# Attention fused with a squared-ReLU MLP: three low bits of every second weight piece on GpSimd, its products on VectorE, a third float32 unit

## The chip, the cores and the metric

The kernel runs on one core of a Trainium2 chip. The metric is the device time of one execution in microseconds (us). Of the kernel before, three runs were timed: 588.53, 588.9 and 590.05 us, with a median of 588.9.

## The reference, cut to what matters

```
scores = q @ k.T / 8;  masked causally;  a = softmax(scores)          # B 4, H 8, S 576, D 64
local  = a @ v
mem    = (phi(q) @ M_prev) / (phi(q) @ z_prev + 1e-6)                 # phi(x) = elu(x) + 1
attn   = g * mem + (1 - g) * local                                    # g = sigmoid(beta), by head
x      = attn as 2304 tokens x 512
out    = (relu(x @ w_in) ** 2) @ w_out                                # 512 -> 2048 -> 512
```

`w_in` and `w_out` come as 64-bit floats and the rest as 32-bit floats. The result is float32.

## The kernel before, in words

**Weights.** The weights are loaded as 32 pieces of 128 rows x 512 columns (`wsrc`, L140 to L146); four pieces of `w_in` and four of `w_out` alternate. Each 64-bit number comes as two 32-bit words. `split_weight` (L156) turns a piece into a float32r high part and a low part in five steps: VectorE shifts the low word right by 29, which leaves its three top bits (L162); ScalarE rebases the exponent of the high word (L163); VectorE shifts that by three and puts the three bits in (L164); ScalarE copies the high part (L167); VectorE subtracts to get the low part (L168). Pieces lie in scratch of their own (`raw`), in two halves of 256 columns (`xw`), or in tiles borrowed from the tokens (`hw`).

**First tokens.** `first_tokens` (L224) computes the first 64 tokens of each of the four batches in two groups. The table `TE` (L65) names the engine of five of its elementwise steps for each group (`d` VectorE, `p` GpSimd): L272, L274, L279, L288 and L294. Each works on 128x512 numbers.

**Attention.** The rest is done in units of one batch and one pair of heads, in an order fixed in `order` (L792). In the first two batches a unit covers two of the four query tiles, afterwards all four. For a unit `loads` (L332) brings keys, queries and values (`kd`, `qm`, `vv`; one buffer of `kd` and one of `vv`). TensorE makes the scores (L465), VectorE adds the mask and takes the row minimum (L484), ScalarE the exponential (L504).
The first `NEF` = 2 units are `full`: TensorE transposes the probabilities in float32 (L519), ScalarE copies them out (L524), and TensorE multiplies them by `vv` in float32 (L563). In all others `vv` is scaled and split into two float16 halves (L398 to L415), the probabilities are split into float16 halves too (L542, L544), a DMA transposes them (L548), and TensorE multiplies in float16 (L569 to L574), after which VectorE adds the halves (L576). L584 adds the memory part, L595 stores to a scratch in DRAM. `TAGS`, `a` and `aT` give the buffers of the split path. The transposes of a `full` unit share their two PSUM buffers (tag `up`) with the MLP.

**MLP.** `moe(n)` (L695) works on a block of 256 tokens in eight steps `j`. A step makes `up` by 24 matmuls of 256 columns (L719 to L721), takes ReLU and square into `r` (one buffer), a high part `gh` (L728 on ScalarE for the first four blocks, L730 on VectorE for the others) and the low part `gl` (L731 on GpSimd), and the step before it multiplies by `w_out` with 12 matmuls of 512 columns (L709 to L711). Block 0 needs the first tokens; the others need their attention rows (`prefetch`, L609). The last two blocks go together in `moe_pair` (L650), with 512 columns and its own `gl` on GpSimd (L677).

**Order.** `ORD` (L79) merges unit 0 with the first 13 weight steps, then units 1 to 3 with the other weight steps and `moe(0)`; the other units and blocks follow. A planner in the framework places the instructions on each engine by its own estimate of their times, so the order within an engine isn't that of the code. Each engine then works its queue in order. All DMAs of the kernel are issued by the queue of SP.

Of the kernel before, what the change touches and what calls it, by code (L numbers as in the profile page):

```python
# [8 lines left out]
F32 = mybir.dt.float32  # L9
F32R = mybir.dt.float32r  # L10
F16 = mybir.dt.float16
BF16 = mybir.dt.bfloat16
U32 = mybir.dt.uint32
AF = mybir.ActivationFunctionType
ALU = mybir.AluOpType
AX = mybir.AxisListType
# [19 lines left out]
PM = 'pd'  # L36
FX = 'dd'
GHN = 4
VMIN = 2.0**-80
NEF = 2  # L40
NES = 6
PXT = 'up'
PXE = 'aa'
# [18 lines left out]
SGROUP = {2: [[(2, 0, 320), (1, 0, 192)]], 1: [], 3: [[(3, 0, 448), (4, 0, 64)]], 4: [[(4, 64, 576)]]}  # L62
STG = [(9, 'hlx'), (8, 'hlx'), (3, 'hlx'), (0, 'hlx')]
XF = 0
TE = ['dd', 'dp', 'pp', 'pp', 'pp']  # L65
TC = 'aa'
TW = 2 * NP * 6 * D
GB = 2
# [21 lines left out]
def fused_kernel(ctx: ExitStack, tc: tile.TileContext, t0_d, zt_d, kk_d, qv_d, beta, w_in, w_out, out):  # L90
    nc = tc.nc
    w_in = w_in.bitcast(U32)
    w_out = w_out.bitcast(U32)
    cp = ctx.enter_context(tc.tile_pool(name="cp", bufs=1))
# [14 lines left out]
        out=mask, in_=mask, pattern=[[-1, MW]], compare_op=ALU.is_ge, fill=-1e30, base=448, channel_multiplier=1  # L109
# [13 lines left out]
    def gates():  # L123
        nc.scalar.activation(gpm, gpm, AF.Exp, scale=-1.0)
        nc.vector.tensor_scalar(out=gpm, in0=gpm, scalar1=1.0, scalar2=None, op0=ALU.add)
        nc.vector.reciprocal(gpm, gpm)
        nc.vector.reciprocal(gi, gm)
        nc.vector.tensor_scalar(out=gm, in0=gm, scalar1=-1.0, scalar2=1.0, op0=ALU.mult, op1=ALU.add)
        nc.vector.reciprocal(gm, gm)
        nc.vector.tensor_scalar(out=gs, in0=gm, scalar1=SC, scalar2=None, op0=ALU.mult)  # L130

        for b in range(GB):
            nc.vector.tensor_copy(gpb[:, b * NP : (b + 1) * NP], gp)
        nc.vector.tensor_scalar(out=g1b, in0=gpb, scalar1=-1.0, scalar2=1.0, op0=ALU.mult, op1=ALU.add)
# [18 lines left out]
    def w_out_op(f, part):  # L153
        return wt[8 * (f // 4) + 4 + f % 4][:, part, :]

    def split_weight(n):  # L156
        for rw, c0, c1 in raw.pop(n):
            rw = rw.rearrange("p (n t) -> p n t", t=2)
            u0, u1 = rw[:, :, 0], rw[:, :, 1]
            f1 = u1.bitcast(F32)  # L160
            hi, lo = wp[n][:, 0, c0:c1], wp[n][:, 1, c0:c1]
            nc.vector.tensor_scalar(out=u0, in0=u0, scalar1=29, scalar2=None, op0=ALU.logical_shift_right)  # L162
            nc.scalar.activation(f1, f1, AF.Prelu, scale=2.0**-111, alpha=-(2.0**32))  # L163
            nc.vector.scalar_tensor_tensor(  # L164
                out=u1, in0=u1, scalar=3, in1=u0, op0=ALU.logical_shift_left, op1=ALU.bitwise_or
            )
            nc.scalar.copy(hi, f1)  # L167
            nc.vector.tensor_tensor(out=lo, in0=f1, in1=hi.bitcast(F32), op=ALU.subtract)  # L168

    def load_weight(n, pool):  # L170
        raw[n] = []
        if pool == "x":
            for c in range(2):
                t = mo.tile([P, DM], F32, tag="x", name="xw", bufs=XB).bitcast(U32)
                raw[n].append((t, c * 256, (c + 1) * 256))
        elif pool in ("h", "l"):
            t = mo.tile([P, NK, BLK], F32, tag="x" + pool, name="hw", bufs=2)
            raw[n].append((t.rearrange("p a b -> p (a b)").bitcast(U32), 0, 512))
        elif pool == "e":
            t = at.tile([P, 2, S], F32, tag="e", name="ew", bufs=EB)  # L180
            raw[n].append((t.rearrange("p a b -> p (a b)").bitcast(U32)[:, :1024], 0, 512))
        else:
            u = wp[n].shape[2] // 512
            raw[n].append((pool.tile([P, 1024 * u], U32, name=f"raw{n}"), 0, 512 * u))
            if u == 2:
# [38 lines left out]
    def first_tokens(tp, ahead):  # L224
        me, ze, se, xe, ye = ([nc.gpsimd if c == "p" else nc.vector for c in t] for t in TE)
        xh = mo.tile([P, NK, BLK], F32R, tag="xh", name="xh", bufs=2)
# [39 lines left out]
        def phi(g):  # L266
# [3 lines left out]
            t2 = tp.tile([P, GN], F32, tag="t2", name="t2", bufs=2)  # L270
            nc.scalar.activation(f, qn, AF.Exp)
            me[g].tensor_scalar(out=f, in0=f, scalar1=1.0, scalar2=None, op0=ALU.min)  # L272
# [8 lines left out]
        def softmax(g):  # L281
# [6 lines left out]
            xe[g].tensor_tensor(out=e, in0=e, in1=t1[:, :, None].to_broadcast(bc), op=ALU.subtract)  # L288
            nc.scalar.activation(e, e, AF.Exp)
            nc.vector.reduce_sum(out=t1, in_=e, axis=AX.X)  # L290
# [38 lines left out]
    dp = ctx.enter_context(tc.tile_pool(name="dp", bufs=1, space=bass.MemoryType.DRAM))  # L329
# [15 lines left out]
    def attention(b, p, tiles, ld, after, early, sfull, full):  # L345
# [31 lines left out]
        w = slice(qa, qb)  # L377
        nc.scalar.activation(pe[:, w], q_raw[:, w], AF.Exp)
        ph = pe if sfull else q_raw
        if PHI and not sfull:  # L380
            nc.scalar.activation(q_raw[:, w], q_raw[:, w], AF.Relu)
            nc.vector.scalar_tensor_tensor(
# [10 lines left out]
        if not full:  # L393
# [10 lines left out]
            nc.vector.tensor_scalar(  # L404
                out=vy, in0=vy, scalar1=VMIN, scalar2=2.0**-VEXP, op0=ALU.max, op1=ALU.mult
            )
# [288 lines left out]
    def moe(n):  # L695
        b, blk = blocks[n]
        xh, xl = xq.pop()
        pend = []
        acc = []

        def down(j, gh, gl):
            if j == 0:
                for t in range(2):
                    acc.append(ps.tile([P, DM], F32, tag="acc", name="oacc", bufs=2))
            last = j == NF // 2 - 1
            for u, t in [(u, t) for t in range(2) for u in range(2)] if last else [(u, t) for u in range(2) for t in range(2)]:
                f = 2 * j + u
                ts = slice(t * P, (t + 1) * P)
                nc.tensor.matmul(acc[t], gh[:, u, ts], w_out_op(f, 0), start=f == 0, stop=False)  # L709
                nc.tensor.matmul(acc[t], gh[:, u, ts], w_out_op(f, 1), start=False, stop=False)  # L710
                nc.tensor.matmul(acc[t], gl[:, u, ts], w_out_op(f, 0), start=False, stop=f == NF - 1)  # L711

        for j in range(NF // 2):
            need(1 + 8 * (j // 2 + 1))
            up = ps.tile([P, 2, BLK], F32, tag="up", name="up", bufs=2)
            for u in range(2):
                f = 2 * j + u
                for k in range(NK):
                    nc.tensor.matmul(up[:, u, :], w_in_op(f, k, 0), xh[:, k, :], start=k == 0, stop=False)  # L719
                    nc.tensor.matmul(up[:, u, :], w_in_op(f, k, 0), xl[:, k, :], start=False, stop=False)  # L720
                    nc.tensor.matmul(up[:, u, :], w_in_op(f, k, 1), xh[:, k, :], start=False, stop=k == NK - 1)  # L721
            r = mo.tile([P, 2, BLK], F32, tag="r", name="r", bufs=RB)
            gh = mo.tile([P, 2, BLK], F32R, tag="gh", name="gh", bufs=GHB)
            gl = mo.tile([P, 2, BLK], F32R, tag="gl", name="gl", bufs=GLB)
            nc.scalar.activation(r, up, AF.Relu, scale=WSC)  # L725
            nc.scalar.activation(r, r, AF.Square)
            if n < GHN:
                nc.scalar.copy(gh, r)  # L728
            else:
                nc.vector.tensor_copy(gh, r)  # L730
            nc.gpsimd.tensor_tensor(out=gl, in0=r, in1=gh.bitcast(F32), op=ALU.subtract)  # L731
            pend.append((j, gh, gl))
            yield
            if n == NBLK - 3 and j in (3, PJ):
                if j == 3:
                    xq.append(pair_tiles())
                pair_prefetch(xq[-1], int(j == PJ))
                yield
            elif j == PJ and n + 1 < NBLK:
                assert n > 0 or last  # L740
                xq.append(prefetch(*blocks[n + 1], *last))
                last.clear()
                yield
            if len(pend) > 1:
                down(*pend.pop(0))
                yield
        for x in pend:
            down(*x)
            yield
        for t in range(2):  # L750
            o = mo.tile([P, DM], F32, tag="x", name="o", bufs=XB)
            nc.scalar.activation(o, acc[t], AF.Copy, scale=WSC)
            if b is None:
                for u in range(2):
                    r0 = (2 * t + u) * S
                    nc.sync.dma_start(out[r0 : r0 + D, :], o[u * D : (u + 1) * D])
            else:
                r0 = b * S + QT[1 + 2 * blk + t][0]
                nc.sync.dma_start(out[r0 : r0 + P, :], o)
        yield  # L760
# [19 lines left out]
    def need(n):  # L780
        while wn[0] < n:
            next(wg)
            wn[0] += 1
# [17 lines left out]
    def attn(i0, i1):  # L801
        for i in range(i0, i1):
# [5 lines left out]

            yield from attention(*order[i], ld, after, i < NEARLY, i < NES, i < NEF and max(order[i][2]) < 4)

# [66 lines left out]
```

## Time and profile before

| | |
|---|---|
| profiled execution | 588.17 us |
| its span, first to last instruction | 586.4 us |
| outside of the span | 1.8 us |
| median of the three timed runs | 588.9 us |
| TensorE busy (matmuls) | 546.1 us, 93% |
| VectorE busy | 386.1 us, 66% |
| ScalarE busy | 348.5 us, 59% |
| GpSimd busy | 122.6 us, 21% |
| mean granted TensorE clock | 0.984 |

Busy time is an average over stages. In the profile's strip of 40 slices TensorE stands at 9 tenths nearly everywhere from the sixth slice on, while VectorE is at 9 in most of the second to the fifth. Matmuls overlap in the records, so a duration there is longer than the distance from one to the next.

### The profile page before, as it was taken

To read this page: it belongs to the slowest core of one execution; us is meant where nothing else is said; L and a number is where in the kernel's file an instruction comes from. 1 tells how busy PE (TensorE), PEld (TensorE's weight loads), DVE (VectorE), ACT (ScalarE), POOL (GpSimd) and SP (SyncE) were. 2 spreads that over 40 slices of the span, in tenths; PEclk is the share of its full clock that TensorE was granted. 3 is DMA by queue.
4 is the path that set the end of the run, shared out by engine and by line. 5 is a ranking of instruction groups with operands and counts; after the bars stand their busy time and mean duration, and the time that the engine had idled before them with its cause. 6 is when DMAs were issued, how large, how long until landed. Compare 5 with 4: busy or idle time off the path is not lost.

```text
span 586.4 us, 11178 instructions
## 1 busy us (share of the span) xinstructions
PE 546.1 (93%) x4006; PEld 471.0 (80%) x4006; DVE 386.1 (66%) x1289; ACT 348.5 (59%) x791; POOL 122.6 (21%) x99
## 2 busy tenths in 40 slices
PE   2468999799999999999999999999999999999996
PEld 2347887588888888888888788888888898888885
DVE  5999989877878687997696687967887211000000
ACT  3789876578867587897566674676656222312222
POOL 2502131124322011121120201111011212122221
PEclk9987999899999999999999999999999999999999
DMA  8967673757645667795553547555253300000001
GB/s 290 409 197 280 222 193 92 165 131 187 133 120 118 152 154 167 147 200 152 126 141 109 125 111 163 116 148 147 69 118 81 108 19 1 36 1 0 2 0 72
DMA packets 127574, 76.24 MB, mean 130 GB/s; under 512 B 99360, under 2 KB 112672, under 8 KB 127520
## 3 DMA queue, kind: packets, MB, share of 16 engines
q1 hardware_dynamic: 127520, 75.55, 48.8%
q8 instruction: 31, 0.51, 0.4%
q14 instruction: 23, 0.19, 0.1%
HBM read 42.63 MB, written 8.78 MB: 88 GB/s over the span
## 4 chain that ended last, share of the span: by engine, by line
PE 64%; DVE 17%; DMA 10%; issue 4%; ACT 3%; SPq 1%; POOL 1%; ACTq 0%; DVEq 0%; POOLq 0%
PE oacc L711 6%; PE oacc L709 6%; PE up L721 6%; PE up L719 6%; PE up L720 6%; PE oacc L710 6%; PE sp L465 5%; DMA aT<-a 4%; DVE w L168 3%; PE up L670 2%; PE up L669 2%; PE up L668 2%; PE acc L574 2%; DMA vv<-in_qv_dram 2%; PE pm L433 2%
## 5 line engine op out<-in xcount | busy, mean ns | idle before, releaser
L731 POOL TENSOR_TENSOR gl<-r,gh 128x512 fp32r<-128x512 f32 x56 | 77.3, 1380 | 332.4 <-ACT gh L728 118.1
L719 PE MATMUL up<-xh,w 128*128 128x256 f32 x448 | 130.1, 290 | 4.1 <-ACT aF L524 4.1
L720 PE MATMUL up<-xl,w 128*128 128x256 f32 x448 | 130.1, 291 | 0.0
L721 PE MATMUL up<-xh,w 128*128 128x256 f32 x448 | 130.0, 290 | 0.0
L504 ACT ACTIVATE e<-e,mx 128x320 f32<-128x320 f32 (+3 forms) x128 | 77.8, 610 | 83.1 <-DVE memx L584 43.0
L719 PEld LDWEIGHTS up<-xh,w 128*128 128x128 f32 x448 | 87.3, 195 | 8.0 <-ACT aF L524 4.5
L709 PE MATMUL oacc<-w,gh 128*128 128x512 f32 x224 | 90.1, 402 | 0.6 <-DVE gh L730 0.6
L720 PEld LDWEIGHTS up<-xl,w 128*128 128x128 f32 x448 | 87.4, 195 | 2.5 <-issue 0.8
L721 PEld LDWEIGHTS up<-xh,w 128*128 128x128 f32 x448 | 87.3, 195 | 2.3 <-issue 1.5
L710 PE MATMUL oacc<-w,gh 128*128 128x512 f32 x224 | 88.7, 396 | 0.0
L711 PE MATMUL oacc<-w,gl 128*128 128x512 f32 x224 | 86.8, 398 | 0.5 <-POOL gl L731 0.4
L544 DVE SCALAR_TENSOR_TENSOR a<-e,a 128x128 f16<-128x128 f32 x120 | 67.8, 583 | 28.2 <-ACT a L542 27.5
L542 ACT ACTIVATE a<-e 128x128 f16<-128x128 f32 x120 | 56.1, 519 | 8.8 <-DMA aT<-a 6.7
L676 DVE CAST gh<-r 128x512 fp32r<-128x512 f32 x16 | 6.9, 428 | 79.3 <-ACT r L675 79.3
L711 PEld LDWEIGHTS oacc<-w,gl 128*128 128x128 f32 x224 | 41.5, 188 | 10.3 <-POOL gl L731 1.8
L484 DVE CUSTOM_DVE_ANT_0 e<-sp,mask 128x320 f32<-128x320 f32 (+3 forms) x128 | 47.8, 418 | 1.4 <-PE sp L465 1.2
L725 ACT ACTIVATE r<-up 128x512 f32<-128x512 f32 x56 | 32.7, 583 | 26.5 <-PE up L721 23.2
L709 PEld LDWEIGHTS oacc<-w,gh 128*128 128x128 f32 x224 | 42.3, 189 | 7.5 <-DVE gh L730 0.8
L710 PEld LDWEIGHTS oacc<-w,gh 128*128 128x128 f32 x224 | 42.3, 189 | 7.4 <-issue 0.7
L674 ACT ACTIVATE r<-up 128x512 f32<-128x512 f32 x16 | 9.6, 599 | 61.8 <-PE up L670 61.8
L574 PE MATMUL acc<-vs,aT 128*128 128x128 f16 x308 | 36.7, 220 | 0.0
L571 PE MATMUL acc<-vs,aT 128*128 128x64 f16 x308 | 35.5, 193 | 0.0
(154 smaller groups left out, 1132.8 us busy)
## 6 DMA issues: line engine op xcount, KB each, us to landing
raw<-in_w_in_dram SPq DMA_DIRECT2D x11, 512.0 KB, 6.7
vv<-in_qv_dram SPq DMA_DIRECT2D x16, 320.0 KB, 3.2
raw<-in_w_out_dram SPq DMA_DIRECT2D x9, 512.0 KB, 7.1
kd<-in_kk_dram SPq DMA_DIRECT2D x16, 288.0 KB, 3.2
out_dram<-o SPq DMA_DIRECT2D x16, 256.0 KB, 2.2
xd<-memx SPq DMA_DIRECT2D x31, 128.0 KB, 2.1
xn<-xd SPq DMA_DIRECT2D x14, 256.0 KB, 2.9
qm<-in_qv_dram SPq DMA_DIRECT2D x8, 321.0 KB, 3.4
```

What stands on the lines that cost most here:

```text
L484: nc.vector.tensor_tensor_reduce(out=e[:, h, ka:kb], in0=sps[:, h, cs], in1=mask[:, 448 - q0 + ka : 448 - q0 + kb], scale=-0.125, scalar=3 ...
L504: ex = nc.scalar.activation(e[:n, h, :ke], e[:n, h, :ke], AF.Exp, bias=bs, scale=-1.0, accum_out=sm[:n, h : h + 1])
L542: nc.scalar.mul(av[:, :, o0 : o0 + w], x, SC)
L544: nc.vector.scalar_tensor_tensor(out=av[:, :, o0 + w : o0 + 2 * w], in0=x, scalar=SC, in1=av[:, :, o0 : o0 + w], op0=ALU.mult, op1=ALU.sub ...
L574: nc.tensor.matmul(o2, aT[:, h * nb + c, :n], vs[:, h, c], start=False, stop=c == i)
L709: nc.tensor.matmul(acc[t], gh[:, u, ts], w_out_op(f, 0), start=f == 0, stop=False)
L710: nc.tensor.matmul(acc[t], gh[:, u, ts], w_out_op(f, 1), start=False, stop=False)
L711: nc.tensor.matmul(acc[t], gl[:, u, ts], w_out_op(f, 0), start=False, stop=f == NF - 1)
L719: nc.tensor.matmul(up[:, u, :], w_in_op(f, k, 0), xh[:, k, :], start=k == 0, stop=False)
L720: nc.tensor.matmul(up[:, u, :], w_in_op(f, k, 0), xl[:, k, :], start=False, stop=False)
L721: nc.tensor.matmul(up[:, u, :], w_in_op(f, k, 1), xh[:, k, :], start=False, stop=k == NK - 1)
L731: nc.gpsimd.tensor_tensor(out=gl, in0=r, in1=gh.bitcast(F32), op=ALU.subtract)
```

## The change

Four things change. The three low bits of the pieces 10, 12, ... 30 are made by GpSimd, from the top 16 bits of the low word, by a multiplication with 2^-13, a minimum with 7 and a conversion to an integer. All the steps of `TE` go to VectorE. The low part `gl` of the blocks 0 to 6 goes from GpSimd to VectorE (`moe_pair` stays). `NEF` is 3, so unit 2 becomes `full`.

```
+U16 = mybir.dt.uint16
+GLV = range(7)
-NEF = 2
+NEF = 3
-TE = ['dd', 'dp', 'pp', 'pp', 'pp']
+TE = ['dd', 'dd', 'dd', 'dd', 'dd']
@@ split_weight
-            nc.vector.tensor_scalar(out=u0, in0=u0, scalar1=29, scalar2=None, op0=ALU.logical_shift_right)
+            if n > 8 and n % 2 == 0:
+                top = rw.bitcast(U16).rearrange("p n (t h) -> p n t h", h=2)[:, :, 0, 1]
+                nc.gpsimd.tensor_scalar(out=u0, in0=top, scalar1=2.0**-13, scalar2=7.0, op0=ALU.mult, op1=ALU.min)
+            else:
+                nc.vector.tensor_scalar(out=u0, in0=u0, scalar1=29, scalar2=None, op0=ALU.logical_shift_right)
@@ moe
-            nc.gpsimd.tensor_tensor(out=gl, in0=r, in1=gh.bitcast(F32), op=ALU.subtract)
+            (nc.vector if n in GLV else nc.gpsimd).tensor_tensor(out=gl, in0=r, in1=gh.bitcast(F32), op=ALU.subtract)
```

## Rows read from the trace of the kernel before

**Rows 1.** Windows: start:end, length, busy us (instructions) by engine, PEclk, DMA share, GB/s.
```profile
core 0: us, PE busy (x) PEld busy (x) DVE busy (x) ACT busy (x) POOL busy (x), PEclk, DMA share, GB/s
30.00:45.00 15.00, 9.87 (x79) 7.33 (x75) 15.00 (x42) 13.61 (x34) 0.96 (x1) 0.78 0.64 213
60.00:75.00 15.00, 15.00 (x97) 13.23 (x97) 15.00 (x40) 13.45 (x36) 3.71 (x3) 1.00 0.83 249
105.00:120.00 15.00, 10.93 (x85) 8.63 (x85) 13.30 (x46) 8.41 (x18) 0.86 (x2) 0.89 0.58 126
225.00:240.00 15.00, 15.00 (x127) 12.77 (x126) 14.50 (x50) 12.88 (x28) 2.65 (x2) 1.00 0.57 139
```

**Rows 2.** Waits of PE: line waited for, releaser, total us, times, longest.
```profile
PE px L303 <- POOL w L294: 6.3, 1, 6.3
PE up L719 <- ACT aF L524: 4.1, 2, 2.5
PE sp L465 <- DVE w L168: 1.0, 1, 1.0
```

**Rows 3.** Timeline of PE, 105 to 114 us: start, us, instruction [idle before it, releaser].
```profile
105.96 0.39 PE L711 MATMUL oacc<-w,gl 128*128 128x512 f32 x1
107.18 1.19 PE L465 MATMUL sp<-kd,qm 64*128 64x448 f32 x8 [0.83 <-DVE mx L484]
...
112.59 1.32 PE L465 MATMUL sp<-kd,qm 64*128 64x512 f32 x4 [3.24 <-DVE mx L484]
113.83 0.58 PE L719 MATMUL up<-xh,w 128*128 128x256 f32 x1
```

**Rows 4.** Timeline of DVE, from unit 2's values to unit 3's result.
```profile
76.79 0.54 DVE L398 TENSOR_REDUCE vx<-vv 128x1 f32<-128x384 f32 x1
...
90.88 0.73 DVE L415 SCALAR_TENSOR_TENSOR vs<-vv,vy,vs 128x192 f16<-128x192 f32 x2
...
104.97 0.82 DVE L398 TENSOR_REDUCE vx<-vv 128x1 f32<-128x640 f32 x1 [2.36 <-DMA vv<-in_qv_dram]
...
107.44 0.75 DVE L576 TENSOR_REDUCE s<-acc 128x128 f32<-128x256 f32 x2
...
112.52 0.68 DVE L625 TENSOR_TENSOR xl<-px,xh 128x512 fp32r<-128x512 f32 x1
```

**Rows 5.** Timeline of SP's queue: issues of the values of units 2 and 3.
```profile
69.59 0.38 SPq L342 DMA_DIRECT2D vv<-in_qv_dram  x1
...
91.68 0.33 SPq L342 DMA_DIRECT2D vv<-in_qv_dram  x1
```

**Rows 6.** Timeline of PE: unit 1 in float32, then unit 2 in float16.
```profile
59.56 0.49 PE L519 MATMUL pxa<-identr,e 128*64 128x128 f32 x3
59.98 1.97 PE L563 MATMUL acc<-vv,aF 64*128 64x64 f32 x12
61.79 0.28 PE L519 MATMUL pxa<-identr,e 128*128 128x128 f32 x1
...
92.65 0.23 PE L569 MATMUL acc<-vs,aT 128*128 128x128 f16 x1
...
93.37 0.36 PE L720 MATMUL up<-xl,w 128*128 128x256 f32 x1
```

**Rows 7.** Groups of DVE by shape: count, busy us, mean ns, idle before.
```profile
L168 DVE TENSOR_TENSOR w<-raw,w 128x512 fp32r<-128x512 f32 x20 | 14.6, 731 | 0.0
L162 DVE TENSOR_SCALAR raw<-raw 128x512 uint32<-128x512 uint32 x20 | 8.9, 451 | 0.4 <-DMA raw<-in_w_in_dram 0.4
L274 DVE TENSOR_TENSOR tr<-tr,w 128x512 f32<-128x512 f32 x1 | 0.7, 672 | 0.0
```

**Rows 8.** Groups of POOL by shape, same columns.
```profile
L731 POOL TENSOR_TENSOR gl<-r,gh 128x512 fp32r<-128x512 f32 x56 | 77.3, 1380 | 332.4 <-ACT gh L728 118.1 <-DVE gh L730 96.3 <-issue 40.0
L387 POOL TENSOR_SCALAR pe<-pe 128x256 f32<-128x256 f32 x6 | 7.3, 1220 | 28.5 <-ACT pe L378 28.5
L288 POOL TENSOR_TENSOR w<-w,t 128x512 f32<-128x512 f32 x2 | 2.6, 1319 | 1.3 <-DVE t L287 1.3
```

**Rows 9.** Timelines of POOL and DVE side by side, where they meet.
```profile
27.03 1.45 DVE L168 TENSOR_TENSOR w<-raw,w 128x512 fp32r<-128x512 f32 x1
...
57.08 1.29 POOL L731 TENSOR_TENSOR gl<-r,gh 128x512 fp32r<-128x512 f32 x1 [1.29 <-ACT gh L728]
...
57.26 1.39 DVE L162 TENSOR_SCALAR hw<-hw 128x512 uint32<-128x512 uint32 x1
...
94.17 1.25 DVE L168 TENSOR_TENSOR w<-hw,w 128x512 fp32r<-128x512 f32 x1
```

## The prediction

> **What bounds the kernel now.** I read the busy time by stage first, then what TensorE waited for, then the timelines of the engines it waited for. The windows show two regimes [rows 1]. From 30 to 45 us VectorE is busy without a gap and TensorE 9.87 of 15 us; from 60 to 75 us both are full. From 105 to 120 us TensorE drops to 10.93 of 15. In the later window TensorE is full again and VectorE near it. So the end is TensorE's work plus its idle time; the page's chain, most of it TensorE's matmuls, says the same. An edit shortens the run only if it takes idle time from TensorE, gives it back a stretch at the low clock, or takes work from it.
>
> Where the idle time lies is read next. Most of it is in the first 60 us, where TensorE waits for VectorE, DMAs and GpSimd, with the wait for GpSimd's `w` the longest piece [rows 2]. Another part is in front of `moe(1)`: TensorE ends block 0 at about 106, waits 0.83 and 3.24 us for VectorE's L484, and starts block 1 at 113.83 [rows 3]. The mean granted clock of that window is 0.89 [rows 1]: with levels of 1.2 and 2.4 GHz this is 3.3 us at the lower, after idling, which costs half of that, 1.65 us. The timeline of VectorE tells why it was late there. Unit 2's values land at about 73 (issued at 69.59), but VectorE, in the middle of the weights, comes to L398 at 76.79 and to the split L415 at 90.88. Only then is the one buffer of `vv` free, and unit 3's values are issued at 91.68 [rows 4, 5]. The next unit's L398 idles VectorE for 2.36 us at 104.97, with unit 3's L576 (107.44) and block 1's `xl` (112.52) queued behind [rows 4].
>
> **The third float32 unit.** For TensorE it is dearer. Unit 1 shows 3 transposes in 0.42 us (0.14 each) and 12 product records in 1.81 us (0.15 each) [rows 6]. A unit has 10 transposes and 20 such records: 1.4 + 3.0 = 4.4 us. What goes is 16 float16 products, 92.65 to 93.37, 0.72 us [rows 6], and the little vt matmul. Net +3.6 us, in a stretch where TensorE is full, so I count all of it. Its transposes also go through the `up` buffers: the two float32 units cost 4.1 us in waits for `aF` [rows 2], 2 us a unit. Unit 2 lies where TensorE has block 0 queued; from 0 to 2.5 us, I take 1.0.
>
> In return it takes L398, L415 and L576 from VectorE (0.54 + 0.73 + 0.75 us [rows 4]), and the four products L544 and some one-column steps which I don't count. More matters that unit 2's product no longer waits for the split. Its values are there at 73, so `vv` can be free at about 75 to 80 instead of 91.68, though what frees it now is TensorE's L563 in place of VectorE. That lets unit 3 run ten us sooner and takes the chain that held L576 and `xl` off block 1. I count the two waits, 0.83 + 3.24 = 4.1 us, the low clock behind them, 1.65, and half of the 1.0 us at 88.8 [rows 2]: −6.2 us together (0 to −6.7). What is late next is TensorE itself with block 0.
>
> **The products that go to VectorE.** `TE` moves seven steps of 128x512. GpSimd needs 1.32 us for one and VectorE 0.67 [rows 7, 8]: +4.7 us on a full VectorE, and about 0.65 less latency for each. But GpSimd's steps also stretch VectorE's. L168 at 27.03 took 1.45 us against 0.68 when undisturbed; it is the last of five such between 15 and 29 us, 3.5 us in all [rows 9]. So throughput loses about 1.2 and the chain to the first transposes, with its 6.3 us wait for GpSimd [rows 2], gains about 0.65 for each of three steps in a row. I take −1.0 (from −3 to +1.5, as the planner may put them behind weights).
>
> `gl` likewise: next to the first, from 57.08, L162 of 57.26 took 1.39 us against 0.45 in its group [rows 7, 9]. Six such rows up to 94.17 cost VectorE 4.9 us; six `gl` at 0.67 to 0.73 on VectorE cost 4.0 to 4.4 [rows 7]. There it is an even exchange, and I count 0. From 120 to 450 us some forty-five more `gl` put about 31 us on VectorE, less what GpSimd's no longer stretch. The window at 225 us has 14.50 of 15 us busy [rows 1] and would be full with two more `gl`. TensorE has the MLP queued to cover attention that comes late, so I take +0.5 (0 to +4).
>
> The Trainium skill (SBUF — State Buffer, "Who interferes with whom") says that GpSimd shares one port pair with VectorE, and a VectorE instruction with two inputs in SBUF, or in a two-port mode, and a GpSimd one that reads SBUF exclude each other for the whole instruction. The trace agrees in the row at 57.26, which ends 0.3 us after GpSimd's. By that rule moving `gl` is free where VectorE is full, as the sum above has it, but the new GpSimd work below is not.
>
> **The low bits on GpSimd.** The eleven pieces make 13 instructions (22 and 28 come in halves): nine of 512 and four of 256 numbers. VectorE loses nine of 0.45 [rows 7] and four of about half that, 5.0 us. The trace has no such GpSimd operation. The nearest is L387, a one-input step of 256 numbers, 1.22 us in the mean [rows 8], dilated by VectorE; a two-input step of 512 takes 1.3 to 1.4 [rows 8]. I put 512 numbers at 1.5 us (0.7 to 2.5) and a half at 0.85: 17 us of GpSimd time between 36 and 90 us, where it is otherwise nearly idle. It isn't on the chain: a piece's L164 also waits for ScalarE. But the six `gl` above cost VectorE 4.9 us for 8.3 us of GpSimd time [rows 8, 9]; at that share 17 us cost 10. Short pieces of the stretch have no such partner, so I take 6, from 2 to 10. VectorE's net is +1 (−3 to +5), and with the 2.0 saved above and more uncounted it comes to about 95 us as now. Cost to TensorE: 0 (−1 to +4).
>
> The Trainium skill (GPSIMD Engine Reference, "Elementwise — side-by-side cycle accounting") has a best case of 769 ns for 512 elements of one input. By that page the estimate would be 9 x 0.77 + 4 x 0.38 = 8.5 us of GpSimd time in place of 17. Row L387 speaks against it, at 1.22 us for 256.
>
> **Sum.** 588.17 us (span 586.4 and 1.8 around it) + 3.6 + 1.0 − 6.2 − 1.0 + 0.5 + 0 = 586.1. The profiled execution is 0.7 below the median of the runs, so on the median it is 586.8; I say 586.5. The difference sits at the edge of what a measurement can tell, 0.3% or 1.8 us.
>
> **Rivals.**
> *The start gains more.* VectorE is full from 15 to 75 us, so whatever frees it moves block 0 forward: if GpSimd's low bits fall beside steps that they don't stretch (cost 2, net −3), and the three steps off the chain give 3, it is 586.1 − 2 − 3 = 581. For it: the 6.3 us wait. Against: +4.7 us of products go the other way. 0.16.
> *It cancels.* Unit 2's 4.6 us on TensorE are paid and only the two waits come back, without the clock and the start: 588.17 + 4.6 − 4.1 = 588.7. 0.20.
> *GpSimd's low bits hold VectorE up: slower.* Place: 36 to 95 us. If each long one costs VectorE its full 1.1 us as the row at 57.26 less its own work does, 13 take 12 us for 5.0 saved; the weights end 5 us later, TensorE stands in block 0 for the last pieces and the waits before block 1 stay in part: 586.1 + 5 = 591. It decides once the low bits take over 1.5 us each or fall onto L164 and L168 throughout. For it: VectorE has no gap before 75 us [rows 1]. Against: the planner can spread them, and L387's delays were small. 0.16.
> *VectorE becomes the bound between 200 and 300 us* with `gl` queued behind attention's long steps; `r` has one buffer, so TensorE would wait for `up`. At 0.1 us for each of the 45 it is 586.1 + 4.5 = 590.6. Against: 7 us lie between two `gl`, and GpSimd's own pace was no faster. 0.07.
>
> **How the numbers follow.** The forecast itself has 0.41, with 584 to 588.5 as its range; two thirds of it are faster by over 0.3%. With all of the first rival that is 0.43, and some 0.05 from the cancelling case: faster 0.48. The same: 0.13 of the forecast, 0.12 of the second and a little of the others, 0.27. Slower 0.25. The range has the bounds of the start below and of the low bits above: 580.5 to 592.
>
> **What would show it.** Unit 3's values issued before 82 us; no float16 products before unit 3; TensorE idle under 1.5 us between 100 and 115 and block 1 begun before 112 at full clock; TensorE's matmuls up by about 3.6 us; L162 on GpSimd near 1.5 us a piece, and VectorE rows above 1 us beside them; L162 and L168 done by about 95. I am wrong if TensorE waits for L168 in block 0, if `aF` costs over 2.5 us, or if idle time of over 2 us appears after 120.

## The result

| | before | after |
|---|---|---|
| median | 590.05 us | 584.02 us |
| range of seven runs each | 588.53 to 591.82 | 580.42 to 586.41 |
| profiled execution (its span) | 588.17 (586.4) | 586.04 (584.3) |
| mean granted clock: before (45 runs, timed beside the experiments), after (7 runs) | 0.981 to 0.988 | 0.987 to 1.000 |

The ratio is 0.990, with a 95% interval of 0.9876 to 0.9923: 6.0 us faster. The forecast was 2.4 us faster, to 586.5, with a range of 580.5 to 592. Direction and range hold; the gain is more than twice the size that was worked out.

The profiled execution is one of the slower runs of after: the two profiles differ by 2.1 us only. The three runs of after at a clock of 0.987 or 0.988 took 585.4 to 586.4 us, the four at 0.993 or above 580.4 to 584.0. The profiles thus show a third of the difference of the medians. Another 2.0 us is how far the profiled run of after lies above its median; it goes with the clock, which was never above 0.988 in a run of before. The last 1.9 us is how far the profiled run of before lies below its own median, and for that no cause is shown.

**The profile after.** Windows, with the columns of [rows 1]:

```profile
0.00:30.00 30.00, 7.26 (x78) 5.77 (x80) 22.93 (x70) 15.08 (x31) 5.25 (x9) 1.00 0.86 311
30.00:60.00 30.00, 25.79 (x198) 21.66 (x195) 26.95 (x67) 23.63 (x57) 18.07 (x7) 0.94 0.76 263
60.00:90.00 30.00, 27.26 (x154) 22.86 (x153) 24.85 (x69) 23.72 (x67) 14.70 (x10) 0.83 0.47 148
90.00:120.00 30.00, 29.77 (x212) 24.77 (x211) 27.67 (x90) 22.01 (x49) 3.49 (x2) 1.00 0.63 166
120.00:450.00 330.00, 327.48 (x2716) 289.74 (x2713) 277.24 (x988) 228.85 (x536) 7.83 (x6) 1.00 0.57 136
```

TensorE's busy time in the same windows of before was 11.12, 22.83, 29.02, 25.19 and 326.22 us. Read as idle time, after loses 3.9 us in the first 30 us, wins 3.0 in the next, loses 1.8 from 60 to 90 and wins 4.6 from 90 to 120, the place in front of block 1. Idle time after 120 falls by 1.3. So the wait that the forecast was built on is gone, and new ones stand ahead of it.

Timeline of TensorE after, where block 0 goes over into block 1 [rows 3]:

```profile
104.64 0.28 PE L725 MATMUL up<-xh,w 128*128 128x256 f32 x1
...
105.71 0.23 PE L575 MATMUL acc<-vs,aT 128*128 128x128 f16 x1
...
106.91 1.19 PE L471 MATMUL sp<-kd,qm 64*128 64x448 f32 x8 [0.23 <-DVE mx L490]
...
115.00 1.13 PE L471 MATMUL sp<-kd,qm 64*128 64x512 f32 x4
116.06 0.38 PE L725 MATMUL up<-xh,w 128*128 128x256 f32 x1
```

Block 1 begins at 116.06, later than the 113.83 of before, but without the waits of 0.83 and 3.24 us and at full clock: unit 3's products and block 0's last steps lie between each other, and TensorE has no gap over a quarter of a microsecond here.

Waits of TensorE after, for the pieces that are new or gone [rows 2]:

```profile
PE sp L471 <- DVE w L174: 10.7, 1, 10.7
...
PE up L725 <- ACT r L731: 2.0, 1, 2.0
PE px L309 <- DVE w L300: 2.0, 1, 2.0
...
PE up L725 <- ACT aF L530: 0.4, 2, 0.2
```

The 6.3 us wait for GpSimd's `w` has become one of 2.0 for VectorE's, and the wait for `aF` fell from 4.1 to 0.4 with three float32 units in place of two. The 10.7 us wait is for the second scores of the program, at 18 us: the new order has them ahead of the first tokens' transposes, and before had them behind. The profile names VectorE's L174 as the last to come, but the keys of these scores are issued at 20.69 and land only at 28.6 us, just before the wait ends. New is also the wait for `r`. Timelines of TensorE, ScalarE and SP's queue after, at that place:

```profile
79.08 0.58 PE L725 MATMUL up<-xh,w 128*128 128x256 f32 x1 [2.05 <-ACT r L731]
```
```profile
75.57 0.70 ACT L169 ACTIVATE raw<-raw 128x512 f32<-128x512 f32 x1 [3.20 <-DMA raw<-in_w_out_dram]
...
77.87 0.67 ACT L169 ACTIVATE raw<-raw 128x512 f32<-128x512 f32 x1 [0.89 <-DMA raw<-in_w_in_dram]
78.43 0.59 ACT L731 ACTIVATE r<-up 128x512 f32<-128x512 f32 x1
```
```profile
71.17 0.81 SPq L198 DMA_DIRECT2D raw<-in_w_in_dram  x2
```

ScalarE stands in order behind L169, a step of a weight piece whose transfer was issued at 71.17. `r` comes behind it, and TensorE waits. The window behind it (same columns) shows what follows:

```profile
78.00:84.80 6.80, 5.72 (x26) 5.50 (x26) 5.24 (x14) 6.80 (x20) 6.32 (x5) 0.50 0.57 229
```

After the idle time TensorE is granted the lower level, 1.2 GHz, for 6.8 us, in which it is busy for 5.72; at the full level that work is half as long, so by an estimate from these two numbers the stretch costs 2.9 us.

### The profile page after: what moved, and what is told of

It reads as the page before. It is cut to its first block, busy times and chain, and to the rows that moved or that the text cites. A ratio compares the mean times of both kernels' runs of the same rounds, so it can differ in the third digit from the quotient of the medians.

```text
span 584.3 us, 11126 instructions
## 1 busy us (share of the span) xinstructions
PE 547.2 (94%) x4019; PEld 474.9 (81%) x4019; DVE 399.4 (68%) x1325; ACT 347.4 (59%) x794; POOL 70.0 (12%) x49
## 4 chain that ended last, share of the span: by engine, by line
PE 72%; DMA 10%; DVE 9%; ACT 6%; issue 1%; SPq 1%; POOL 1%; ACTq 0%; DVEq 0%
PE up L725 7%; PE up L726 7%; PE up L727 7%; PE oacc L717 7%; PE oacc L715 7%; PE oacc L716 7%; PE sp L471 6%; DMA qm<-in_qv_dram 3%; PE up L675 2%; PE up L674 2%; DMA aT<-a 2%; PE up L676 2%; PE acc L580 2%; PE pm L439 2%; DVE e L490 2%
## 5 line engine op out<-in xcount | busy, mean ns | idle before, releaser
L717 PE MATMUL oacc<-w,gl 128*128 128x512 f32 x224 | 85.4, 397 | 0.3 <-DVE gl L737 0.3
L550 DVE SCALAR_TENSOR_TENSOR a<-e,a 128x128 f16<-128x128 f32 x116 | 64.1, 565 | 24.0 <-ACT a L548 23.9
L683 POOL TENSOR_TENSOR gl<-r,gh 128x512 fp32r<-128x512 f32 x16 | 20.6, 1290 | 380.9 <-DVE gh L682 380.9
L548 ACT ACTIVATE a<-e 128x128 f16<-128x128 f32 x116 | 54.5, 523 | 4.2 <-DMA aT<-a 4.0
L737 DVE TENSOR_TENSOR gl<-r,gh 128x512 fp32r<-128x512 f32 x56 | 38.8, 693 | 5.7 <-ACT gh L734 5.1
```

What stands on the lines that cost most here:

```text
L548: nc.scalar.mul(av[:, :, o0 : o0 + w], x, SC)
L550: nc.vector.scalar_tensor_tensor(out=av[:, :, o0 + w : o0 + 2 * w], in0=x, scalar=SC, in1=av[:, :, o0 : o0 + w], op0=ALU.mult, op1=ALU.sub ...
L737: (nc.vector if n in GLV else nc.gpsimd).tensor_tensor(out=gl, in0=r, in1=gh.bitcast(F32), op=ALU.subtract)
```

## The experiments

The forecast's theory: unit 2 in float32 takes the waits before block 1 away, and the engine moves weigh little. The rivals: the gain is that of one of the moves; or it is the order of the instructions, which the planner makes anew for any edit, and which belongs to no part of the change.

### One part undone, with the order that the planner makes

Each is the changed kernel with one line set back.

```
e1_no_unit   -NEF = 3                                      +NEF = 2
e2_no_gl     -GLV = range(7)                               +GLV = range(0)
e3_no_te     -TE = ['dd', 'dd', 'dd', 'dd', 'dd']          +TE = ['dd', 'dp', 'pp', 'pp', 'pp']
e4_no_low    -if n > 8 and n % 2 == 0:                     +if n > 99 and n % 2 == 0:
```

> The change with NEF = 2 again, everything else of it kept. Theory of the prediction (the third float32 unit frees the values early and so takes the waits in front of block 1 away): the gain of 6 us on the medians goes, 588 to 591 us, and 3 to 4 us of idle time of TensorE come back between 100 and 115 us. Rival (GpSimd's products stretched VectorE's, and moving them is the gain): 581 to 584 us, since 3.6 us of TensorE work go.

> The change with gl of blocks 0 to 6 on GpSimd again. Theory of the prediction (even exchange): within 1.5 us of the changed kernel, 582.5 to 585.5 us. Rival (GpSimd's products stretch VectorE's steps, 4.9 us up to 94 us and 11 us after 120 us): 587 to 590 us.

> The change with the five steps of the first tokens back on their engines of before. Theory of the prediction (1.0 us gained by moving them): 584 to 586 us. Rival (GpSimd's steps at the start cost VectorE 3.5 us and TensorE the 6.3 us wait): 587 to 590 us. Third view, from the idle time of TensorE in the first 30 us, which is 3.8 us longer in the changed kernel than before: the moved steps lose there, 580 to 583 us.

> The change with all low bits on VectorE again. Theory of the prediction (13 steps on GpSimd save VectorE 5.0 us and cost it 6): 583 to 585 us. Rival one (GpSimd has the bits for nothing, since its steps of one input hardly stretch VectorE's): 586 to 589 us, VectorE being short in 15 to 75 us. Rival two (the bits come late, 2.2 to 3.0 us for a piece, and hold up the weights): 580 to 583 us.

| | median (range), us | ratio to before |
|---|---|---|
| e1_no_unit | 593.73 (593.25 to 594.48) | 1.0062 (1.0046 to 1.0078) |
| e2_no_gl | 602.05 (599.38 to 603.68) | 1.0195 (1.0171 to 1.0220) |
| e3_no_te | 596.62 (595.83 to 597.72) | 1.0107 (1.0089 to 1.0125) |
| e4_no_low | 589.01 (585.80 to 591.25) | 0.9984 (0.9966 to 1.0001) |

In time all four miss, e4_no_low by a hair: its first rival had 586 to 589 us. What e1_no_unit was to show in the trace did come: TensorE is idle for 3.6 us between 100 and 115 us, against 0.2 after. Undoing any part costs 5 to 18 us, 45 us together, where all parts give 6. Parts of a plain sum can't behave so. What all four share is a new order, and the next experiments test whether that makes them slow.

### The same work in another order

Two kernels with the changed kernel's work on the same engines: one weight in `ORD`, which merges unit 0 with the first weight steps, is set to 20 or to 16.

```
-    merge((attn(1, FIRST), 52), (wsteps(33), 20), (first(), 18))
+    merge((attn(1, FIRST), 52), (wsteps(33), 20), (first(), 20))    # e8_other_order; 16 in e12_third_order
```

> The changed kernel with one number of the merge changed (block 0 as 20 parts in place of 18), so that all the work is the same on the same engines, and the planner makes another order. Theory one (the parts make the time): 582 to 586 us. Theory two (the order makes it): off by 4 us or more, 588 to 602 us.

> The changed kernel with block 0 merged as 16 parts in place of 18: the same work on the same engines in a third order of the planner. Theory two: anywhere between 582 and 602 us, and off the changed kernel by over 2 us. Theory one: 582 to 586 us.

e8_other_order took 595.59 us (592.38 to 596.61), a ratio of 1.0085 (1.0058 to 1.0111); e12_third_order 586.29 (582.64 to 587.41), 0.9919 (0.9892 to 0.9945). Theory two holds for both. So the order by itself turns the change from 6 us faster into 5 us slower than before. It is e8 that shows this: the interval of e12 overlaps that of after. Windows of e8_other_order, where it loses:

```profile
90.00:120.00 30.00, 29.25 (x218) 24.47 (x218) 26.88 (x86) 21.91 (x49) 3.27 (x2) 1.00 0.61 163
120.00:450.00 330.00, 320.24 (x2586) 279.87 (x2585) 264.82 (x937) 220.16 (x517) 6.65 (x6) 0.99 0.57 132
```

In front of block 1 it is as good as after. It loses 7.2 us of busy time between 120 and 450 us. Timelines of TensorE and VectorE in e8_other_order at one of these places:

```profile
235.36 0.39 PE L716 MATMUL oacc<-w,gh 128*128 128x512 f32 x1
237.60 0.99 PE L717 MATMUL oacc<-w,gl 128*128 128x512 f32 x2 [1.85 <-DVE vx L406]
```
```profile
234.99 0.82 DVE L404 TENSOR_REDUCE vx<-vv 128x1 f32<-128x640 f32 x1 [1.66 <-DMA vv<-in_qv_dram]
235.73 1.22 DVE L550 SCALAR_TENSOR_TENSOR a<-e,a 128x1024 f16<-128x1024 f32 x1
236.86 0.68 DVE L737 TENSOR_TENSOR gl<-r,gh 128x512 fp32r<-128x512 f32 x1
```

VectorE has `gl` (L737) queued behind L404, which waits for a transfer. TensorE's product of `gl` waits with it, though the profile names L406 as the last to come. On GpSimd no step that waits for `vv` stands before it. This is the prediction's fourth rival, and it is real at this place, in an order that puts `gl` there: the groups of VectorE, here and in after, have L404's long form with 13.7 and 5.9 us of idle time ahead of it. It isn't the whole of the loss. Of the 9.8 us for which TensorE is idle between 120 and 450 us here, this wait is 1.85, and two waits for a transfer of attention rows (`xn`, L625) make 3.1. And e2_no_gl, with `gl` on GpSimd in its own order, is idle for 9.0 us there.

```profile
L404 DVE TENSOR_REDUCE vx<-vv 128x1 f32<-128x640 f32 x16 | 13.1, 816 | 13.7 <-DMA vv<-in_qv_dram 13.7
```
```profile
L404 DVE TENSOR_REDUCE vx<-vv 128x1 f32<-128x640 f32 x16 | 13.0, 814 | 5.9 <-DMA vv<-in_qv_dram 5.8
```

### One part undone, in the order of after

To keep an order, the sequence of instructions that the planner had made was written into the kernel, and each engine's instructions were chained in it:

```
for k in order:
    ins = traced[k]
    e = str(ins.engine)
    if e in before:
        tc.add_manual_dep(ins, before[e], AFTER, ...)
    before[e] = ins.name
```

The edits are those of e2, e3 and e4, with that chain. In the traces TensorE and ScalarE work the same sequence of instructions in all three as after. The chain alone, with the changed kernel's own work, was not run.

> The change with gl of blocks 0 to 6 on GpSimd again, as in the second experiment, but every engine works its instructions in the order of the changed kernel: the planner's order is written out and kept. Theory one (the work on GpSimd costs the 18 us): 599 to 604 us. Theory two (the 18 us come from the order that the planner made anew): 583 to 588 us, as the moved products take 1.3 in place of 0.7 us and TensorE has one step in between.

> The change with the steps of the first tokens on their engines of before, as in the third experiment, and the changed kernel's order kept on every engine. Theory one (these seven steps cost the 12.6 us): 594 to 598 us. Theory two (the order does): 582 to 587 us, up to 2 us for seven steps of 0.65 us more each in the chain of the start.

> The change with all low bits on VectorE, as in the fourth experiment, and the changed kernel's order kept on every engine. Theory one (the bits on GpSimd gain the 5 us): 587 to 590 us. Theory two (the order does): 582 to 586 us, VectorE taking 5.0 us more and GpSimd's 2.2 to 3.0 us a piece going.

| | median (range), us | ratio to before |
|---|---|---|
| e5_no_gl_kept_order | 581.92 (581.07 to 583.93) | 0.9873 (0.9853 to 0.9893) |
| e6_no_te_kept_order | 586.42 (583.88 to 587.84) | 0.9938 (0.9916 to 0.9959) |
| e7_no_low_kept_order | 583.19 (578.21 to 585.54) | 0.9878 (0.9842 to 0.9913) |

The same three edits that cost 5 to 18 us above now move the time by −2.1 to +2.4 us against 584.02 (by the ratios, −1.6 to +2.2). The last two fit theory two; e5 is 1.1 us faster than its range. `gl` and the low bits are, if anything, better where they were, and the first tokens' products look better on VectorE. Each of the three intervals still overlaps that of after.

### The moves and the order apart

One kernel has all three moves with `NEF` = 2 and the order of before. Another has the third unit and the order of after with no move. A third is the second with `TE` on VectorE.

```
e9_moves_in_order_before   NEF = 2, GLV = range(7), TE all 'd', low bits on GpSimd; order of before
e10_unit_in_order_after    NEF = 3, GLV = range(0), TE as before, low bits on VectorE; order of after
e11_order_unit_tokens      e10 with TE all 'd'
```

> The kernel before with the three moves between GpSimd and VectorE (first tokens, gl, low bits), NEF = 2, every engine in the order of the kernel before. Theory two (the order makes the time, the moves little): 587 to 591 us against 590 of before. Theory one (the moves are the gain): 582 to 586 us.

> The third float32 unit and the changed kernel's order, with all three moves undone (first tokens, gl and low bits on the engines of before). Theory two: 583 to 587 us, as the single undoings in that order gave -2, +2.4 and -0.8 us. Theory one: 595 us or more, as all of the moves' gain would go.

> What the experiments in the kept order point to as best: the changed kernel's order and float32 unit, the first tokens on VectorE, gl on GpSimd and all low bits on VectorE. Theory two with the parts additive: 581 us (579 to 583). If they are not: 582 to 585 us, as the changed kernel. Theory one: 600 us or more.

| | median (range), us | ratio to before |
|---|---|---|
| e9_moves_in_order_before | 589.59 (586.89 to 591.53) | 0.9985 (0.9965 to 1.0005) |
| e10_unit_in_order_after | 585.26 (584.06 to 587.16) | 0.9915 (0.9897 to 0.9933) |
| e11_order_unit_tokens | 582.82 (580.54 to 583.83) | 0.9867 (0.9849 to 0.9885) |

The third unit with its order gives 0.85% (5.0 us) without any move; the moves give 0.15% in the order of before, and 0.15% on top of e10 in that of after (0.9915 to 0.9900), neither told apart from nothing. Of the moves only `TE` shows: e10 to e11 is 0.48%, 2.8 us, and the intervals don't overlap. e11 and e5 have the lowest ratios of all, 0.3% below that of after; their intervals overlap with its. All three kernels fit theory two, e11 its range with the parts additive. Waits of TensorE in e10 and in e11 show where `TE` acts:

```profile
PE sp L471 <- DMA kd<-in_kk_dram: 11.0, 1, 11.0
...
PE px L309 <- POOL w L300: 4.3, 2, 3.6
```
```profile
PE sp L471 <- DMA kd<-in_kk_dram: 10.7, 1, 10.7
...
PE px L309 <- DVE w L300: 1.8, 1, 1.8
```

The wait for the first tokens' weights is shorter by 2.5 us, nearly all of the 2.8. The long wait at 18 us is the order's, whatever engine makes the products, and here it is the keys' transfer that ends it.

What `gl` on VectorE costs stands in the traces, one profiled execution of each kernel. Window of e11_order_unit_tokens, with `gl` on GpSimd:

```profile
120.00:450.00 330.00, 329.46 (x2721) 291.63 (x2720) 268.64 (x947) 230.43 (x536) 63.26 (x49) 1.00 0.60 138
```

TensorE is idle for 0.5 us there, and for 0.7 and 0.6 in e5 and e10, which have `gl` on GpSimd too. With the same order and `gl` on VectorE it is 2.5, 2.3 and 3.4 us (after, e6, e7). So the move costs some 2 us of idle time. In the order of before it is 3.8 us with `gl` on GpSimd and 5.7 with all three moves (before, e9), which agrees.

Timelines of TensorE and VectorE in e9_moves_in_order_before [rows 3, 4]:

```profile
107.91 1.19 PE L471 MATMUL sp<-kd,qm 64*128 64x448 f32 x8 [1.32 <-DVE mx L490]
113.31 1.13 PE L471 MATMUL sp<-kd,qm 64*128 64x512 f32 x4 [3.24 <-DVE mx L490]
```
```profile
91.16 0.88 DVE L421 SCALAR_TENSOR_TENSOR vs<-vv,vy,vs 128x192 f16<-128x192 f32 x2
...
105.69 0.82 DVE L404 TENSOR_REDUCE vx<-vv 128x1 f32<-128x640 f32 x1 [1.73 <-DMA vv<-in_qv_dram]
```

All three moves are there, and the 3.24 us wait with its late split stands where it stood. In e10_unit_in_order_after it is gone (windows of that kernel):

```profile
90.00:120.00 30.00, 28.67 (x185) 23.23 (x184) 26.84 (x85) 22.19 (x47) 7.39 (x5) 1.00 0.59 160
```

The same window sorts all the kernels of this case. With `NEF` = 3, in six orders, TensorE is busy for 28.67 to 30.00 of the 30 us from 90 to 120, at a clock of 0.99 or 1.00 (eleven kernels). With `NEF` = 2, in two orders, it is 24.79 to 25.19 at 0.89 or 0.94 (before, e1, e9). e1_no_unit has an order of its own, and its window is as poor:

```profile
90.00:120.00 30.00, 24.80 (x149) 19.65 (x150) 28.49 (x96) 20.47 (x46) 2.84 (x2) 0.89 0.63 167
```

Its waits are others, though, as the next section shows. The unit's own price in one and the same order is left open. It wasn't tried with `NEF` = 2 in the order of after, nor `NEF` = 3 in that of before: the order of either needs unit 2's values where the other form of the unit doesn't have them yet.

## Why the prediction was right in direction, and where its size failed

**The third unit: the waits went, but not by the route that was forecast, and the term was too small.** The forecast had −1.6 us for it (+3.6 + 1.0 − 6.2); unit and order together measure −5.0 (e10 against before, −3.9 to −6.1). By its terms:
- *TensorE's work*, +3.6: its busy time rose by 1.1 us (546.1 to 547.2). In the windows at 1.2 GHz before was busy for 14.5 us and after for 12.5, which doubles the time of the work in them; with half of that difference the work rose by some 2.1. Right in kind, too high by 1.5.
- *Waits for `aF`*, +1.0: they fell from 4.1 to 0.4 us. This step failed. I took 2 us a unit from before and halved it; but the wait belongs to the order and not to the unit: it is 0.2 to 0.6 us in the order of after and 3.5 in e2, with three units in each.
- *The waits before block 1*, −4.1 of the −6.2: they went, in every kernel with the unit. How they went is not as forecast. Unit 3's values are issued at 87.15, not before 82, 4.5 us sooner than in [rows 5]; block 1 begins at 116.06, not before 112. TensorE is full there while unit 3's products and block 0's last steps lie between each other, not because block 1 is sooner. The step of the forecast that failed is that values freed early take the waits away: by the rows below that is neither enough nor needed. e1, without the unit and in its own order, issues unit 3's values sooner than after, and TensorE still waits 3.00 us for their split. e2, with the unit and in its own order, issues them later than before did, and TensorE is busy for all of the 30 us. What the unit does for TensorE there is not settled.
- *The clock*, −1.65 of the −6.2: this is the term that was mis-sized most. I counted the 3.3 us in front of block 1 and left the rest of the low clock in the profile of before as it was: its clock was 0.984, in runs 0.981 to 0.988. In e10 it is 0.986 to 0.999. Taking twice the missing share of 586 us as the time at the lower level, the middle run of before (0.985) spends 18 us there and that of e10 (0.9965) 4. TensorE was busy for 14.5 of 17.0 us at that level in the profile of before, so 14 us less of it is worth, by this estimate, 14 x 0.85 / 2 = 6 us: as large as the whole gain, and paid in part for what e10 loses at its start. For after, whose middle run has 0.993 and so 8 us at the lower level, the same estimate gives 4 us. A high clock alone doesn't make a kernel fast: e4 has 0.990 to 1.000 and 589.01 us.

Queue of SP in after, in e1_no_unit and in e2_no_gl, unit 3's values, and then TensorE in e1_no_unit:

```profile
87.15 0.33 SPq L348 DMA_DIRECT2D vv<-in_qv_dram  x1
```
```profile
85.40 0.33 SPq L348 DMA_DIRECT2D vv<-in_qv_dram  x1
```
```profile
93.59 0.33 SPq L348 DMA_DIRECT2D vv<-in_qv_dram  x1
```
```profile
101.49 0.26 PE L575 MATMUL acc<-vs,aT 128*128 128x128 f16 x1 [3.00 <-DVE vs L421]
```

**The start**, −1.0 (−3 to +1.5): in a kept order `TE` on VectorE is worth −2.4 (e6 back to after) and −2.8 us (e10 to e11): right in sign, near the gainful end. The first rival, "the start gains more", has its reason here. Against it stands the 10.7 us wait, by which the window from 0 to 30 us lost 3.9 us to the new order.

**`gl` and the low bits**, +0.5 and 0: in a kept order both together cost 1.9 us (e11 to after, 0.9867 to 0.9900), within the intervals of nothing. The bounds held (0 to +4 and −1 to +4). For `gl` the traces have about 2 us of idle time, as shown above, so its +0.5 was too small.

**How the low bits came out.** I put 512 numbers at 1.5 us and the cost to VectorE at 6 us for 17 of GpSimd. Groups of GpSimd after [rows 8]:

```profile
L166 POOL TENSOR_SCALAR raw<-raw 128x512 uint32<-128x512 uint16 x5 | 14.8, 2969 | 23.2 <-DMA raw<-in_w_out_dram 15.4 <-DVE raw L170 7.5
...
L166 POOL TENSOR_SCALAR hw<-hw 128x512 uint32<-128x512 uint16 x4 | 8.9, 2213 | 13.9 <-DVE mx L490 13.7
L166 POOL TENSOR_SCALAR xw<-xw 128x256 uint32<-128x256 uint16 x4 | 5.7, 1424 | 0.5 <-DVE w L174 0.2
```

The GpSimd time is 29.4 us, not 17. Yet VectorE pays less for it than was forecast. Timelines of GpSimd and VectorE side by side [rows 9]:

```profile
46.96 7.00 POOL L166 TENSOR_SCALAR raw<-raw 128x512 uint32<-128x512 uint16 x3
```
```profile
47.08 0.87 DVE L394 SCALAR_TENSOR_TENSOR pe<-qm,pe 128x256 f32<-128x256 f32 x1
...
50.15 0.67 DVE L174 TENSOR_TENSOR w<-raw,w 128x512 fp32r<-128x512 f32 x1
...
52.00 0.88 DVE L168 TENSOR_SCALAR raw<-raw 128x512 uint32<-128x512 uint32 x1
...
63.94 1.17 DVE L174 TENSOR_TENSOR w<-raw,w 128x512 fp32r<-128x512 f32 x1
```

Most of VectorE's steps with two inputs take 0.67 to 0.69 us beside it, as alone [rows 7]. But L394 took 0.87 us against 0.41 to 0.42 in its other five rows, and L174 at 63.94, beside another low-bit step, 1.17. Over all thirteen steps eight rows of VectorE are longer than others of their form, by 0.2 to 0.5 us each and 3.3 us in all. Up to 110 us such rows stand only beside GpSimd's work. The forecast had 6 us of cost for 5.0 saved; it came to 3.3. The third rival had each long one cost VectorE 1.1 us; none does. The weights are later all the same: their last VectorE step ends at 107.5 us, not at about 95, since the new order puts them there, and TensorE doesn't wait for them. Two errors, a duration too short and a cost to VectorE for each us of it too high, cancelled in part.

The Trainium skill (SBUF — State Buffer, "Who interferes with whom") has the loser of the shared port blocked for the whole instruction. The two-input `gl` of [rows 9] agrees. The one-input L166 does not, since a step of over 2 us costs VectorE 0.5 us at most: here the measurement decides.

**What the method missed.** All terms were changes to the order of before. The prediction named the planner once, as a bound of one term, and gave its order no case of its own. By e8 and e12 the same work comes out at 586 and 596 us; a rival "the new order loses elsewhere, 120 to 450 us" with the price of some 10 us was due, and the chance of slower was rather low for that. That this change got a good order is not something that the profile of before could tell. Of the six orders with three float32 units two ran faster than before (after, e12), one the same (e4) and three slower (e2, e3, e8), so that the direction came out right was in part luck.

## What to carry to other kernels

Where a planner orders the instructions, an edit is two changes: the work and the order. Undoing parts one at a time measures the order with them; chain the engines in one order before asking what a part is worth, and try a few orders of the same work before keeping or dropping it. A step moved to an in-order engine must be looked up in that engine's queue: `gl` on VectorE costs TensorE most where it stands behind a step that waits for a transfer.

## What the runs showed of the hardware that I had not expected

A one-input GpSimd step can be stretched to four times its length beside a busy VectorE, and costs VectorE little. Timeline of GpSimd after, L393 with 256 float32 numbers:

```profile
16.35 3.43 POOL L393 TENSOR_SCALAR pe<-pe 128x256 f32<-128x256 f32 x1 [13.96 <-ACT pe L384]
...
43.91 0.85 POOL L393 TENSOR_SCALAR pe<-pe 128x256 f32<-128x256 f32 x1 [2.79 <-ACT pe L384]
...
83.16 0.85 POOL L393 TENSOR_SCALAR pe<-pe 128x256 f32<-128x256 f32 x1
```

Timeline of VectorE beside these three:

```profile
17.79 0.68 DVE L294 TENSOR_TENSOR w<-w,t 128x512 f32<-128x512 f32 x1
18.39 0.68 DVE L280 TENSOR_TENSOR tr<-tr,w 128x512 f32<-128x512 f32 x1
...
43.93 0.66 DVE L325 TENSOR_TENSOR xl<-xp,xh 128x512 fp32r<-128x512 f32 x1
...
83.35 0.75 DVE L737 TENSOR_TENSOR gl<-r,gh 128x512 fp32r<-128x512 f32 x1 [0.46 <-ACT gh L734]
```

At 16.35 VectorE works without a gap through steps with both inputs in SBUF, and L393 ends 0.7 us after the last of them. At 43.91 VectorE is as busy, but its input `xp` is in PSUM, and L393 takes 0.85 us. At 83.16 a single step with both inputs in SBUF lies beside it, and L393 takes 0.85 us as well. So one such step does not hold it, and an unbroken row of them did; no run parts what decides.
